# Attention with scores made twice: GpSimd sums all key chunks, a one-term score tile, moved rows of maxima, a front in three banks

## The chip, the cores and the metric

The kernel runs on 1 core of one Trainium2 chip. The metric is device time in microseconds (us) of one execution, shown as the median of several runs. The profile is one further execution with the hardware profiler on. Engines carry the profile's names: PE (TensorE), PEld (its weight loads), DVE (VectorE), ACT (ScalarE), POOL (GpSimd), SP (SyncE, which issues the transfers here).

## The reference

Attention with pooled queries, then a mixture of experts with Sinkhorn gating, then a soft mixture of experts. The change touches the attention alone:

```python
B, H, S, D = q.shape                       # 4, 8, 1152, 64
q_pool = q.reshape(B, H, S // 2, 2, D).mean(axis=3)
scores = (1.0 / np.sqrt(D)) * np.matmul(q_pool, k.transpose(0, 1, 3, 2))
scores = scores - np.max(scores, axis=-1, keepdims=True)
attn = np.exp(scores)
attn = attn / (np.sum(attn, axis=-1, keepdims=True) + 1e-09)
return np.matmul(attn, v)
```

## The kernel before, in words

There are 32 heads in 16 pairs. One head has 576 pooled queries and 1152 keys (9 chunks of 128). Scores are made twice. The first time (`emit_S`, queries on partitions, 384 keys a tile) serves only to find each query's maximum: a matmul, then a DVE maximum. A pair needs 9 query tiles: tile x = 0 holds the last 64 pooled queries of both heads, tiles 1 to 4 the others of one head, 5 to 8 those of the second; each takes three matmul groups. `emit_nm` negates and joins the three partial maxima; `emit_row` turns them by matmuls against the identity into a row that ACT copies into `q2`. The second time (`emit_E`, keys on partitions) scores of one chunk come out with the maximum already subtracted (two matmuls per half, one with `q1`, one with `q2`), and ACT takes the exponential into `e`. `emit_PV` multiplies by the values. The denominator is the sum of `e` over chunks (adds on POOL into `acc`, L223 and L225) and then over partitions (`emit_sum`: matmuls with ones).

Values are split into a rounded part and a remainder. `k_bank` transposes four chunks of keys, ACT copies the rounded part (L133), DVE subtracts for the remainder (L134); `q_bank` does so for queries (L104, L113, L115). `kq8` does the ninth chunk of keys and the last 64 queries, and fills `qd`, the weights of tile x = 0. `kd_dma` and `q2_dma` copy pieces to other partitions through SP's queue.

The order of work is written by hand (`manual_schedule`): a loop over slots, one chunk of one head each, 9 a head, 18 a pair (`u` is the slot within a pair, `nxt` and `nn` the pairs one and two ahead). Each slot makes exponentials for the present head and one score tile for a later one; even slots add the values' product of two chunks and a second score tile. Preparation of the coming pair, sums, rows and reciprocals hang at fixed `u`. All engines take their instructions in that order.

PSUM: two banks for the score tiles S, three for `se` (scores before the exponential), one bank `t` shared by all transposes, rows and sums (`bank()`), two for the product.

After slot 287 the experts' part begins, which this change does not touch.

Of the kernel before, what the change touches and what calls it, by code (L numbers as in the profile page):

```python
# [23 lines left out]
def attention(ctx, nc, tc, q, k, v, xa, ident, ones, hooks):  # L24
# [27 lines left out]

    qd = [kq_p.tile([128, 2, 128], F32R, name=f"qd{u}") for u in range(2)]

# [25 lines left out]
    def load_v(pi):  # L80
# [38 lines left out]
    def k_bank(pi, c0, n, ps):  # L119
        st = prep.setdefault(pi, {})  # L120
        if c0 == 0:
            st["kp"] = kq_p.tile([128, 2, 1152], F32R, tag="kp", name="kp")

            st["q1"] = kq_p.tile([128, 2, 2, 288], F32R, tag="q1", name="q1", bufs=2)
            st["q2"] = kq_p.tile([128, 2, 2, 288], F32R, tag="q2", name="q2", bufs=2)
        kr = raws["k"][pi]
        for c in range(n):
            nc.tensor.transpose(
                ps[:, c * 128:(c + 1) * 128], kr[:, c0 + c].rearrange("p h d -> p (h d)"), ident
            )  # L130
# [13 lines left out]
    def kq8(pi):  # L144
        ps = bank()
        k_bank(pi, 8, 1, ps)
        q_tr(pi, 8, 1, ps, 128)
        o, st = qd[pi % 2], prep[pi]
        xs = [(slice(64 * h, 64 * h + 64), slice(128 + 64 * h, 192 + 64 * h)) for h in range(2)]
        src = ps[:, 128:256].rearrange("p (h g x) -> p h g x", h=2, g=2)  # L150
        q1 = st["q1"][:, :, :, 256:]
        nc.scalar.copy(q1, src)
        for x, y in xs:
            nc.scalar.copy(o[x, 0, x], ps[x, y])
# [4 lines left out]
        for x, y in xs:  # L159
            nc.vector.tensor_tensor(out=o[x, 1, x], in0=ps[x, y], in1=o[x, 0, x].bitcast(F32), op=ALU.subtract)  # L160

# [8 lines left out]
    def q2_dma(pi):  # L170
        st = prep[pi]
        nc.sync.dma_start(out=st["q2"][0:64].bitcast(F32), in_=st["q1"][0:64].bitcast(F32))


    def emit_S(ph, x, n):
# [4 lines left out]
        if x == 0:  # L180
            mm = [(qd[pi % 2][:, z], st["kp"][:, 0]) for z in range(2)]
        else:
            g, u = divmod(x - 1, 2)
            mm = [(st["q1"][:, h, g, 128 * u:128 * u + 128], KD[ph % 3][:, 0])]
        ps = ps_s.tile([128, 512], F32, tag="S", name="S")[:, :384]
        for z, (w, r) in enumerate(mm):
            nc.tensor.matmul(ps, lhsT=w, rhs=r[:, 384 * n:384 * n + 384], start=z == 0, stop=z == len(mm) - 1)  # L187
        nc.vector.tensor_reduce(out=M_[ph][:, x, n:n + 1], in_=ps, axis=AX.X, op=ALU.max)  # L188
# [20 lines left out]
    def emit_E(ph, c):  # L209
# [11 lines left out]
        if c == 1:  # L221
            acc_[ph] = sm_p.tile([128, 2, 288], F32, tag="acc", name="acc")
            nc.gpsimd.tensor_tensor(out=acc_[ph], in0=E_[ph, 0], in1=e, op=ALU.add)  # L223
        elif 1 < c < 8:
            nc.gpsimd.tensor_tensor(out=acc_[ph], in0=acc_[ph], in1=e, op=ALU.add)  # L225

    def emit_PV(ph, c):
# [3 lines left out]
        for g in range(2):  # L231
# [3 lines left out]
            )  # L235
        if c < 8:
            E_.pop((ph, c))

    def emit_sum(ph):
        ps = bank()  # L240
        for z, t in enumerate((acc_.pop(ph), E_.pop((ph, 8)))):
            for g in range(2):
                nc.tensor.matmul(
                    ps[64 * g:64 * g + 64, :288], lhsT=ones[:, :64], rhs=t[:, g], start=z == 0, stop=z == 1
                )
        R_[ph] = sm_p.tile([128, 288], F32, tag="rs", name="rs")
# [18 lines left out]
    load_k(0)  # L265
    load_q(0)
    k0(0)
    k4(0)
    pool_q(0, 0)
    pool_q(0, 1)  # L270
    kq8(0)
    with tc.issue_after(kd_dma(0, 0)):
        load_k(1)
        kd_dma(0, 1)
        load_v(0)
# [8 lines left out]

    first(3)
    q_bank(0, 0)
    q_bank(0, 1)
    q2_dma(0)
    emit_nm(0, 0, 1)
    emit_row(0, 0, 1)  # L290
    first(12)
    pool_q(1, 0)
    pool_q(1, 1)
    emit_nm(0, 1, 4)
    k0(1)
    first()
    emit_row(0, 1, 4)

    for s in range(SLOTS * NPH + 9):
# [37 lines left out]
        if ph and c in (5, 6):  # L339
            emit_recip(ph - 1, c - 5)  # L340
        if ph + 1 < NPH:
            if u == 8 and ph + 2 < NPH:
                emit_nm(ph + 2, 0, 1)
            if u == 10:
                emit_row(ph + 1, 0, 1)
            if u in (6, 16):
                emit_nm(ph + 1, 1, 4)
            if u in (8, 17):
                emit_row(ph + 1, 1, 4)
        if ph and c == 7:  # L350
# [769 lines left out]
```

## Time and profile before

| | us |
|---|---|
| median of 3 runs | 2327.2 (2326.01 to 2327.26) |
| the profiled execution's own time | 2326.89 |
| span of its trace | 2324.9 |
| first exponential's scores begin (PE) | 33.31 |
| last sum of the attention begins (PE) | 607.88 |

The attention fills the first quarter of the span, the experts the rest. The page gives busy time for each engine over the whole span, so an average over unlike stages; the timeline gives, for each instruction, its start, its length and the engine's idle time before it with what ended it. Matmuls overlap, so on PE the distance from start to start says what an instruction costs.

### The profile page before, as it was taken

To read this page: it belongs to the slowest core of one execution; us is meant where nothing else is said; L and a number is where in the kernel's file an instruction comes from. 1 tells how busy PE (TensorE), PEld (TensorE's weight loads), DVE (VectorE), ACT (ScalarE), POOL (GpSimd) and SP (SyncE) were. 2 spreads that over 40 slices of the span, in tenths; PEclk is the share of its full clock that TensorE was granted. 3 is DMA by queue.
4 is the path that set the end of the run, shared out by engine and by line. 5 is a ranking of instruction groups with operands and counts; after the bars stand their busy time and mean duration, and the time that the engine had idled before them with its cause. 6 is when DMAs were issued, how large, how long until landed. Compare 5 with 4: busy or idle time off the path is not lost.

```text
span 2324.9 us, 41275 instructions
## 1 busy us (share of the span) xinstructions
PE 2218.8 (95%) x16965; PEld 1986.0 (85%) x16965; DVE 1446.5 (62%) x2692; ACT 843.0 (36%) x1779; POOL 538.8 (23%) x336
## 2 busy tenths in 40 slices
PE   6999999989999999999999999999999999999996
PEld 4666666666699999999999999999999999988863
DVE  5666666766667686686568558657755865622321
ACT  3454545544443442233334224223323423312212
POOL 4666666665500030030012003002100300100000
PEclk9999999999999999999999999999999999999998
DMA  7444354444121221121121212212211211221169
GB/s 169 104 101 118 92 122 109 92 109 136 32 74 46 91 91 56 55 100 56 64 82 65 73 55 83 82 40 88 82 46 64 92 64 56 103 98 55 55 221 313
DMA packets 121195, 211.40 MB, mean 91 GB/s; under 512 B 43696, under 2 KB 95408, under 8 KB 109744
## 3 DMA queue, kind: packets, MB, share of 16 engines
q1 hardware_dynamic: 121008, 208.77, 29.6%
q8 instruction: 134, 2.20, 0.4%
q14 instruction: 53, 0.43, 0.1%
HBM read 161.56 MB, written 14.16 MB: 76 GB/s over the span
## 4 chain that ended last, share of the span: by engine, by line
PE 59%; issue 8%; DVE 7%; ACT 1%; DMA 0%; POOL 0%; SPq 0%; DVEq 0%; ACTq 0%; POOLq 0%
PE g L550 9%; PE g L551 9%; PE g L552 9%; PE y L579 7%; PE y L577 7%; PE y L578 7%; DVE ho L539 2%; DVE ht L532 2%; PE y L649 1%; DVE v L470 1%; PE y L651 1%; PE y L650 1%; DVE acc L587 1%; PE se L216 1%; PE o L232 1%
## 5 line engine op out<-in xcount | busy, mean ns | idle before, releaser
L550 PE MATMUL g<-xs,w 128*128 128x256 f32 x2304 | 659.6, 286 | 0.0
L552 PE MATMUL g<-xs,w 128*128 128x256 f32 x2304 | 653.7, 284 | 1.0 <-DVE w L445 1.0
L551 PE MATMUL g<-xs,w 128*128 128x256 f32 x2304 | 654.0, 284 | 0.0
L577 PE MATMUL y<-v,ho 128*128 128x256 f32 x1764 | 503.3, 285 | 9.1 <-ACT ho L538 9.1
L579 PE MATMUL y<-v,ho 128*128 128x256 f32 x1764 | 503.2, 285 | 7.1 <-DVE ho L539 7.1
L578 PE MATMUL y<-v,ho 128*128 128x256 f32 x1764 | 502.1, 285 | 0.0
L550 PEld LDWEIGHTS g<-xs,w 128*128 128x128 f32 x2304 | 444.6, 193 | 7.7 <-issue 7.0
L552 PEld LDWEIGHTS g<-xs,w 128*128 128x128 f32 x2304 | 444.2, 193 | 1.2 <-DVE w L445 1.2
L551 PEld LDWEIGHTS g<-xs,w 128*128 128x128 f32 x2304 | 444.5, 193 | 0.3
L566 ACT ACTIVATE hr<-g 128x512 f32<-128x512 f32 x252 | 150.5, 597 | 772.6 <-PE g L552 753.5
L532 DVE TENSOR_TENSOR ht<-hr 128x512 f32<-128x512 f32 x315 | 230.1, 764 | 223.5 <-ACT hr L566 221.1
L577 PEld LDWEIGHTS y<-v,ho 128*128 128x128 f32 x1764 | 341.2, 193 | 10.4 <-ACT ho L538 10.4
L579 PEld LDWEIGHTS y<-v,ho 128*128 128x128 f32 x1764 | 341.8, 194 | 8.5 <-DVE ho L539 8.5
L445 POOL TENSOR_TENSOR w<-stg,w 128x1024 fp32r<-128x1024 f32 x28 | 68.1, 2433 | 1193.1 <-ACT w L444 1193.1
L578 PEld LDWEIGHTS y<-v,ho 128*128 128x128 f32 x1764 | 341.5, 194 | 0.0
L188 DVE TENSOR_REDUCE m<-S 128x1 f32<-128x384 f32 x432 | 235.2, 551 | 144.4 <-PE S L187 132.7
L587 DVE SCALAR_TENSOR_TENSOR acc<-y,P,acc 128x256 f32<-128x256 f32 x540 | 244.4, 477 | 117.4 <-PE y L579 117.4
L225 POOL TENSOR_TENSOR acc<-acc,e 128x576 f32<-128x576 f32 x192 | 273.7, 1425 | 98.7 <-ACT e L219 91.7
L539 DVE TENSOR_TENSOR ho<-ht,ho 128x512 fp32r<-128x512 f32 x315 | 258.5, 821 | 7.0 <-ACT ho L538 6.9
L219 ACT ACTIVATE e<-se 128x288 f32<-128x288 f32 x576 | 206.7, 410 | 144.3 <-PE se L216 141.3
L216 PE MATMUL se<-q,kd 128*128 128x288 f32 x1152 | 223.5, 311 | 15.7 <-ACT q L206 15.2
L538 ACT CAST ho<-ht 128x512 fp32r<-128x512 f32 x315 | 188.8, 618 | 81.3 <-DVE ht L532 78.6
(180 smaller groups left out, 2421.4 us busy)
## 6 DMA issues: line engine op xcount, KB each, us to landing
xs<-xd SPq DMA_DIRECT2D x63, 1024.0 KB, 4.8
stg<-in_moe_w_dram SPq DMA_DIRECT2D x60, 512.0 KB, 5.9
kd<-kp SPq DMA_DIRECT2D x32, 576.0 KB, 5.7
m2w<-in_moe_w_dram SPq DMA_DIRECT2D x13, 1024.0 KB, 10.4
m2w<-in_moe_w_dram SPq DMA_DIRECT2D x22, 512.0 KB, 8.7
kr<-in_k_dram SPq DMA_DIRECT2D x32, 288.0 KB, 6.4
qr<-in_q_dram SPq DMA_DIRECT2D x16, 576.0 KB, 3.8
kd<-kp SPq DMA_DIRECT2D x32, 288.0 KB, 3.2
```

What stands on the lines that cost most here:

```text
L188: nc.vector.tensor_reduce(out=M_[ph][:, x, n:n + 1], in_=ps, axis=AX.X, op=ALU.max)
L216: nc.tensor.matmul(ps, lhsT=kd[:, z, 128 * c:128 * c + 128], rhs=y[:, h, g], start=z == 0, stop=z == 1)
L225: nc.gpsimd.tensor_tensor(out=acc_[ph], in0=acc_[ph], in1=e, op=ALU.add)
L532: nc.vector.tensor_tensor(out=src, in0=q[0], in1=q[1], op=op)
L539: nc.vector.tensor_tensor(out=o[:, 1], in0=src, in1=o[:, 0].bitcast(F32), op=ALU.subtract)
L550: nc.tensor.matmul(o, lhsT=w[:, 0, kk, c], rhs=x[:, 0, kk], start=kk == 0, stop=False)
L551: nc.tensor.matmul(o, lhsT=w[:, 0, kk, c], rhs=x[:, 1, kk], start=False, stop=False)
L552: nc.tensor.matmul(o, lhsT=w[:, 1, kk, c], rhs=x[:, 0, kk], start=False, stop=kk == 3)
L577: nc.tensor.matmul(ps, lhsT=o[:, 0, c], rhs=v[:, 0, c], start=c == 0, stop=False)
L578: nc.tensor.matmul(ps, lhsT=o[:, 0, c], rhs=v[:, 1, c], start=False, stop=False)
L579: nc.tensor.matmul(ps, lhsT=o[:, 1, c], rhs=v[:, 0, c], start=False, stop=c == 3)
L587: nc.vector.scalar_tensor_tensor(out=y, in0=ps, scalar=p, in1=y, op0=ALU.mult, op1=ALU.add)
```

## The change

- `qd` keeps only the rounded part: tile x = 0 is one matmul instead of two, and two DVE subtractions a pair go.
- In `kq8` the query transpose comes before the copies of the key part of the bank instead of after them.
- The ninth chunk's `e` is added into `acc` by POOL too; `emit_sum` is two matmuls instead of four.
- `emit_row` stands right behind the slot's exponentials and first score tile, instead of at the slot's end.
- `k0`, `k4` move from u = 14, 16 to 13, 15, `q_bank(nxt, 0)` from 5 to 6 (first pair: `kq8` to 3, `k0(1)`, `k4(1)` into slots 1 and 2).
- In the front the first pair's banks come from the three `se` banks; queries are pooled first, both `q_bank`s come before the score tiles, all 15 tiles of head 0 come before its rows, and `q2_dma` and both `kd_dma` are issued before the next pair's loads.

The order in which the engines get their work, by program text. PE, slots 7 to 9 of a pair (`se` scores of a chunk, `S` score tiles, `o` values' product, `t<-identr,nm` the row of maxima). Before:

```order
L187 MATMUL S<-kp,qd_123 128x384 x2
L216 MATMUL se<-q_2218,kd_126 128x288
...
L187 MATMUL S<-kp,qd_123 128x384 x2
L232 MATMUL o<-e,vr 64x288 x4
L187 MATMUL S<-kp,qd_123 128x384 x2
L200 MATMUL t<-identr,nm_125 128x128 x4
L216 MATMUL se<-q_2218,kd_127 128x288
L216 MATMUL se<-q_2219,kd_127 128x288
```

With the change:

```order
L189 MATMUL S<-kp,qd_123 128x384
L218 MATMUL se<-q_2166,kd_126 128x288
...
L189 MATMUL S<-kp,qd_123 128x384
L202 MATMUL t<-identr,nm_125 128x128 x4
L234 MATMUL o<-e,vr 64x288 x4
L189 MATMUL S<-kp,qd_123 128x384
L218 MATMUL se<-q_2166,kd_127 128x288
L218 MATMUL se<-q_2167,kd_127 128x288
```

The row moved ahead of the values' product and of one score tile, and each tile of x = 0 is one matmul.

DVE, slots 5 to 8 of a pair (`q<-t,q` the remainder of a bank of queries, `m` maxima of a score tile, `nm` their join, `rs` reciprocals). Before:

```order
L115 TENSOR_TENSOR q_2218<-t,q_2218 64x256 x2
L251 RECIPROCAL rs<-rs 128x144
L188 TENSOR_REDUCE m_2289<-S 128x1 x2
L251 RECIPROCAL rs<-rs 128x144
L191 TENSOR_REDUCE nm_125<-m_2289 128x4
L188 TENSOR_REDUCE m_2469<-S 128x1
```

With the change:

```order
L250 RECIPROCAL rs<-rs 128x144
L190 TENSOR_REDUCE m_2251<-S 128x1
L120 TENSOR_TENSOR q_2166<-t,q_2166 64x256 x2
L190 TENSOR_REDUCE m_2251<-S 128x1
L250 RECIPROCAL rs<-rs 128x144
L193 TENSOR_REDUCE nm_125<-m_2251 128x4
L190 TENSOR_REDUCE m_2427<-S 128x1
```

The queries' remainder moved behind the first reciprocal and one maximum; the join `nm` stands where it stood.

POOL, one pair (`acc` sums of `e`, `qp` the pooled queries of the pair after next). Before:

```order
L100 TENSOR_TENSOR qp<-qr 128x9x64 x2
L223 TENSOR_TENSOR acc<-e 128x576
L225 TENSOR_TENSOR acc<-acc,e 128x576 x6
L223 TENSOR_TENSOR acc<-e 128x576
L225 TENSOR_TENSOR acc<-acc,e 128x576 x6
```

With the change:

```order
L105 TENSOR_TENSOR qp<-qr 128x9x64 x2
L225 TENSOR_TENSOR acc<-e 128x576
L227 TENSOR_TENSOR acc<-acc,e 128x576 x7
L225 TENSOR_TENSOR acc<-e 128x576
L227 TENSOR_TENSOR acc<-acc,e 128x576 x7
```

The ninth chunk's add now stands ahead of the pooling of queries.

The diff, cut to its core:

```diff
-    qd = [kq_p.tile([128, 2, 128], F32R, name=f"qd{u}") for u in range(2)]
+    qd = [kq_p.tile([128, 128], F32R, name=f"qd{u}") for u in range(2)]
...
+    front = [True]
     def bank():
+        if front[0]:
+            return ps_e.tile([128, 512], F32, tag="se", name="t")
         return ps_t.tile([128, 512], F32, tag="t", name="t")
...
+        if n == 1:
+            q_tr(pi, 8, 1, ps, 128)
         o = st["kp"][:, 0, c0 * 128:(c0 + n) * 128]
...
         k_bank(pi, 8, 1, ps)
-        q_tr(pi, 8, 1, ps, 128)
...
-        for x, y in xs:
-            nc.vector.tensor_tensor(out=o[x, 1, x], in0=ps[x, y], in1=o[x, 0, x].bitcast(F32), op=ALU.subtract)
...
-        for z, (w, r) in enumerate(mm):
-            nc.tensor.matmul(ps, lhsT=w, rhs=r[:, 384 * n:384 * n + 384], start=z == 0, stop=z == len(mm) - 1)
+        nc.tensor.matmul(ps, lhsT=w, rhs=r[:, 384 * n:384 * n + 384], start=True, stop=True)
...
-        elif 1 < c < 8:
+        elif c > 1:
             nc.gpsimd.tensor_tensor(out=acc_[ph], in0=acc_[ph], in1=e, op=ALU.add)
...
-        for z, t in enumerate((acc_.pop(ph), E_.pop((ph, 8)))):
-            for g in range(2):
-                nc.tensor.matmul(
-                    ps[64 * g:64 * g + 64, :288], lhsT=ones[:, :64], rhs=t[:, g], start=z == 0, stop=z == 1
-                )
+        t = acc_.pop(ph)
+        for g in range(2):
+            nc.tensor.matmul(ps[64 * g:64 * g + 64, :288], lhsT=ones[:, :64], rhs=t[:, g], start=True, stop=True)
...
     load_q(0)
+    pool_q(0, 0)
+    pool_q(0, 1)
     k0(0)
     k4(0)
-    pool_q(0, 0)
-    pool_q(0, 1)
     kq8(0)
-    with tc.issue_after(kd_dma(0, 0)):
+    kd_dma(0, 0)
+    q_bank(0, 0)
+    q_bank(0, 1)
+    with tc.issue_after(q2_dma(0)):
+        kd_dma(0, 1)
         load_k(1)
-        kd_dma(0, 1)
...
-    first(3)
-    q_bank(0, 0)
-    q_bank(0, 1)
-    q2_dma(0)
+    first(15)
     emit_nm(0, 0, 1)
+    emit_nm(0, 1, 4)
     emit_row(0, 0, 1)
-    first(12)
+    emit_row(0, 1, 4)
+    front[0] = False
+    first()
...
         first()
+        if ph + 1 < NPH:
+            if u in (8, 17):
+                emit_row(ph + 1, 1, 4)
+            if u == 10:
+                emit_row(ph + 1, 0, 1)
         if on and nxt < NPAIR:
-            if s == 0:
-                k4(1)
-            if u == (2 if s < 9 else 1):
+            if s in (1, 2):
+                (k0, k4)[s - 1](1)
+            if u == (3 if s < 9 else 1):
...
-            elif u == 5:
+            elif u == 6:
                 q_bank(nxt, 0)
...
-            if u == 14:
+            if u == 13:
                 k0(nn)
-            elif u == 16:
+            elif u == 15:
                 k4(nn)
```

## Rows read from the trace of the kernel before

**Rows 1.** The page, part 1: busy us, share of the span, instructions of each engine.
```profile
PE 2218.8 (95%) x16965; PEld 1986.0 (85%) x16965; DVE 1446.5 (62%) x2692; ACT 843.0 (36%) x1779; POOL 538.8 (23%) x336
```

**Rows 2.** Stretches: start:end, length, busy us (count) by engine, PEclk, DMA share, GB/s.
```profile
33.31:609.00 575.69, 530.36 (x3428) 369.39 (x3428) 379.77 (x814) 289.04 (x775) 358.45 (x253) 1.00 0.44 106
540.00:545.00 5.00, 4.46 (x18) 2.63 (x19) 1.97 (x6) 1.40 (x3) 1.37 (x2) 0.66 0.00 0
```

**Rows 3.** Timeline of one pair, PE: start us, length, line, count [idle before, releaser].
```profile
285.47 0.34 PE L216 MATMUL se<-q,kd 128*128 128x288 f32 x1
...
300.07 0.70 PE L216 MATMUL se<-q,kd 128*128 128x288 f32 x4
301.17 0.62 PE L187 MATMUL S<-kp,qd 128*128 128x384 f32 x2 [0.40 <-DVE m L188]
302.15 0.51 PE L187 MATMUL S<-kp,qd 128*128 128x384 f32 x2
...
304.56 0.34 PE L216 MATMUL se<-q,kd 128*128 128x288 f32 x1
305.40 0.67 PE L216 MATMUL se<-q,kd 128*128 128x288 f32 x3 [0.49 <-ACT q L206]
...
311.42 0.66 PE L243 MATMUL t<-acc,ones 128*64 128x288 f32 x4
311.90 0.66 PE L243 MATMUL t<-e,ones 128*64 128x288 f32 x4
...
321.12 0.63 PE L200 MATMUL t<-identr,nm 128*128 128x128 f32 x4 [0.56 <-DVE nm L191]
321.59 0.34 PE L216 MATMUL se<-q,kd 128*128 128x288 f32 x1
...
325.29 0.27 PE L128 MATMUL t<-ident,kr 128*128 128x128 f32 x1
326.52 0.30 PE L104 MATMUL t<-ident,qp 128*128 128x128 f32 x1 [0.95 <-DVE kp L134]
```

**Rows 4.** Timeline of the same pair, DVE, POOL and ACT.
```profile
298.69 0.77 DVE L115 TENSOR_TENSOR q<-t,q 64x256 fp32r<-64x256 f32 x2 [0.50 <-ACT q L113]
...
301.50 1.04 DVE L251 RECIPROCAL rs<-rs 128x144 f32<-128x144 f32 x1
...
302.46 0.11 DVE L191 TENSOR_REDUCE nm<-m 128x4 fp32r<-128x12 f32 x1
...
317.60 2.90 POOL L225 TENSOR_TENSOR acc<-acc,e 128x576 f32<-128x576 f32 x2 [0.55 <-ACT e L219]
...
320.16 0.71 ACT L219 ACTIVATE e<-se 128x288 f32<-128x288 f32 x2 [1.17 <-PE se L216]
...
320.47 2.78 POOL L100 TENSOR_TENSOR qp<-qr 128x576 f32<-128x576 f32 x2
```

**Rows 5.** Timeline of the front, SP and PE.
```profile
12.40 0.50 SPq L166 DMA_DIRECT2D kd<-kp  x1
...
22.31 0.95 PE L187 MATMUL S<-kd,q 128*128 128x384 f32 x2
...
32.40 1.11 PE L200 MATMUL t<-identr,nm 128*128 128x128 f32 x4 [1.12 <-DVE kp L134]
```

**Rows 6.** The page, part 6: transfers, KB each, median us from issue to landing.
```profile
kd<-kp SPq DMA_DIRECT2D x32, 576.0 KB, 5.7
```

**Rows 7.** Timeline of the attention's end, POOL and PE.
```profile
601.78 5.88 POOL L225 TENSOR_TENSOR acc<-acc,e 128x576 f32<-128x576 f32 x4 [0.75 <-ACT e L219]
...
607.88 0.66 PE L243 MATMUL t<-acc,ones 128*64 128x288 f32 x4
```

**Rows 8.** Groups by line and shape, 0 to 640 us: busy us, mean ns | idle before.
```profile
L461 POOL TENSOR_TENSOR vs<-vb 128x1024 f32<-128x1024 f32 x1 | 3.3, 3345 | 0.0
L461 POOL TENSOR_TENSOR va<-vb,va 128x1024 f32<-128x1024 f32 x1 | 2.4, 2403 | 0.1
L100 DVE TENSOR_TENSOR qp<-qr 128x576 f32<-128x576 f32 x2 | 1.4, 750 | 0.0
```

More of the change, by code (lines that the diff above doesn't have):

```diff
@@ L146, in kq8 @@
         k_bank(pi, 8, 1, ps)
-        q_tr(pi, 8, 1, ps, 128)
         o, st = qd[pi % 2], prep[pi]
-        xs = [(slice(64 * h, 64 * h + 64), slice(128 + 64 * h, 192 + 64 * h)) for h in range(2)]
         src = ps[:, 128:256].rearrange("p (h g x) -> p h g x", h=2, g=2)
         q1 = st["q1"][:, :, :, 256:]
+        for h in range(2):
+            nc.scalar.copy(o[64 * h:64 * h + 64, 64 * h:64 * h + 64], ps[64 * h:64 * h + 64, 128 + 64 * h:192 + 64 * h])
         nc.scalar.copy(q1, src)
-        for x, y in xs:
-            nc.scalar.copy(o[x, 0, x], ps[x, y])
         for h in range(2):
@@ L158, in kq8 @@
             )
-        for x, y in xs:
-            nc.vector.tensor_tensor(out=o[x, 1, x], in0=ps[x, y], in1=o[x, 0, x].bitcast(F32), op=ALU.subtract)
     def kd_dma(pi, h):
@@ L171, in q2_dma @@
         st = prep[pi]
-        nc.sync.dma_start(out=st["q2"][0:64].bitcast(F32), in_=st["q1"][0:64].bitcast(F32))
+        return nc.sync.dma_start(out=st["q2"][0:64].bitcast(F32), in_=st["q1"][0:64].bitcast(F32)).ins
     def emit_S(ph, x, n):
@@ L180, in emit_S @@
         if x == 0:
-            mm = [(qd[pi % 2][:, z], st["kp"][:, 0]) for z in range(2)]
+            w, r = qd[pi % 2], st["kp"][:, 0]
         else:
             g, u = divmod(x - 1, 2)
-            mm = [(st["q1"][:, h, g, 128 * u:128 * u + 128], KD[ph % 3][:, 0])]
+            w, r = st["q1"][:, h, g, 128 * u:128 * u + 128], KD[ph % 3][:, 0]
         ps = ps_s.tile([128, 512], F32, tag="S", name="S")[:, :384]
-        for z, (w, r) in enumerate(mm):
-            nc.tensor.matmul(ps, lhsT=w, rhs=r[:, 384 * n:384 * n + 384], start=z == 0, stop=z == len(mm) - 1)
+        nc.tensor.matmul(ps, lhsT=w, rhs=r[:, 384 * n:384 * n + 384], start=True, stop=True)
         nc.vector.tensor_reduce(out=M_[ph][:, x, n:n + 1], in_=ps, axis=AX.X, op=ALU.max)
@@ L235, in emit_PV @@
             )
-        if c < 8:
-            E_.pop((ph, c))
+        E_.pop((ph, c))
     def emit_sum(ph):
         ps = bank()
-        for z, t in enumerate((acc_.pop(ph), E_.pop((ph, 8)))):
-            for g in range(2):
-                nc.tensor.matmul(
-                    ps[64 * g:64 * g + 64, :288], lhsT=ones[:, :64], rhs=t[:, g], start=z == 0, stop=z == 1
-                )
+        t = acc_.pop(ph)
+        for g in range(2):
+            nc.tensor.matmul(ps[64 * g:64 * g + 64, :288], lhsT=ones[:, :64], rhs=t[:, g], start=True, stop=True)
         R_[ph] = sm_p.tile([128, 288], F32, tag="rs", name="rs")
@@ L283, in first @@
                 emit_S(*firsts.pop(0))
-    first(3)
-    q_bank(0, 0)
-    q_bank(0, 1)
-    q2_dma(0)
+    first(15)
     emit_nm(0, 0, 1)
+    emit_nm(0, 1, 4)
     emit_row(0, 0, 1)
-    first(12)
+    emit_row(0, 1, 4)
+    front[0] = False
+    first()
     pool_q(1, 0)
     pool_q(1, 1)
[L294 to L297, printed above, removed]
     for s in range(SLOTS * NPH + 9):
@@ L340, in attention @@
             emit_recip(ph - 1, c - 5)
[L341 to L349, printed above, removed]
+        if u == 8 and ph + 2 < NPH:
+            emit_nm(ph + 2, 0, 1)
+        if u in (6, 16) and ph + 1 < NPH:
+            emit_nm(ph + 1, 1, 4)
         if ph and c == 7:
```

## The prediction

> **What bounds the kernel now.** The page comes first: PE is busy for 95% of the span [rows 1], but that mixes the experts, which are not touched, with the attention. So I cut out the attention: in 575.69 us PE is busy 530.36, DVE 379.77, POOL 358.45, ACT 289.04 [rows 2]. PE leads there and yet is not full, and no other engine is near its limit. A stage like this is read from one pair in the timeline. A pair takes 321.59 - 285.47 = 36.12 us [rows 3]. On PE the instructions stand head to tail except at five places, and these are what the reader should look for: a score tile that waits for DVE's maxima (301.17), two waits for ACT's copy of the row (305.40, and the same again behind 321.59), a row that waits for the joined maxima (321.12) and the ninth query transpose, which waits until DVE has read another part of the same bank (326.52) [rows 3]. So the attention's time is PE's work plus these waits, and each edit is worth what it takes from one or the other. I count from start to start, since the ends of matmuls are modelled; four `se` matmuls stand (0.70 - 0.34) / 3 = 0.12 us apart [rows 3].
>
> **The sum, term by term.** It is made against the profiled execution, 2326.9 us, which lies 0.3 below the median.
>
> 1. *Sums of two matmul groups instead of four.* The first half starts at 311.42, the second at 311.90 [rows 3]: 0.48 us of PE for each head goes, 32 x 0.48 = **-15.4**. The price is one more add on POOL (term 4).
> 2. *Tile x = 0 with one matmul.* Two take 0.51 us, and a single one's length in that pair is 0.34 by the same model (two start 0.17 apart) [rows 3]. Three a pair; the first pair's lie in the front, where other things decide. 45 x 0.17 = **-7.7**. The two DVE subtractions that go with it lie in idle time of DVE: nothing.
> 3. *Ninth query transpose ahead of the copies.* From the key transpose to the query transpose 326.52 - 325.29 = 1.23 us pass; back to back I take 0.12, as for `se`. 15 x 1.11 = **-16.7**.
> 4. *The add ahead of the pooling.* That transpose reads the pooled queries, so term 3 holds only if POOL is there in time. Now the last add of the odd head ends at 317.60 + 2.90 = 320.50 and the pooling runs to 323.25. With the change the ninth add can start when ACT has the last exponential, 320.16 + 0.71 = 320.87; 1.45 for the add (2.90 for two) and 2.78 for the pooling end it at 325.10 [rows 4]. The query transpose could start at 325.29 + 0.12 = 325.41 [rows 3]. A cover of 0.3 us: I take **0**. Bounds: 0, and the whole of term 3 (+16.7) where POOL is 1.4 us late. This also says what a shorter wait at 321.12 would bring: PE would reach the transpose early and wait for POOL there.
> 5. *Row at u = 8 ahead of the values' product.* From 304.56 to 305.40 are 0.84 us instead of 0.12: with the product of two chunks between row and use, ACT's copy is hidden. 16 x 0.72 = **-11.5**. The row at u = 17 stays right before its use, and that wait stays.
> 6. *Queries' bank at u = 6 instead of 5.* The tile at 301.17 waits because DVE sat 0.50 us for ACT's copy (298.69) and then did subtraction and reciprocal before the maxima [rows 4]. With the reciprocal first, that idle time goes. From the four matmuls at 300.07 the next would start after about 0.53; it started after 1.10: 15 x 0.57 = **-8.6**. Bounds: 0 and this.
> 7. *A new wait, in the row at u = 8.* Its old place was behind the product; its new one is just behind the slot's score tile: 302.15 less 0.57 (term 6) less one 0.17 (term 2), plus the tile's own 0.17, about 301.6. The joined maxima are ready at 302.46 + 0.11 = 302.57 [rows 4], less the 0.50 of idle time that goes, 302.07. So PE waits about 0.5, and the product and the next tile queue behind the row: 15 x 0.5 = **+7.5**. Bounds: 0, and 1.04 more (one reciprocal, the instruction ahead of the join [rows 4]).
> 8. *`k0` and `k4` a slot earlier.* I looked whether the wait at 321.12 goes. DVE has the same two subtractions, two reciprocals and maxima between the tile of slot 14 and the join, only in another order, and runs through them without a pause; the row's place on PE doesn't move either. **0**. Bounds: -0.56 x 15 = -8.4, most of which POOL would take back (term 4), and +3.
> 9. *The front.* Tiles from x = 1 on need the second copy of keys to other partitions, issued 12.40 to 12.90 [rows 5]; with 5.7 us to landing [rows 6] it is there at about 18.1. Before, these tiles began at 22.31 because both banks of queries stood between. With the change the banks come first and the tiles begin as soon as the copy lands: 4.2 earlier. The head's rows no longer wait 1.12 us for the next pair's keys (32.40) [rows 5]; in return those keys' transposes, about as long as the row's 1.11, are paid inside slot 1. Together **-4**. Bounds: 0 (the queue lands the copy later, since the order of loads changed) and -6.
> 10. *The end.* POOL's adds for the last head run without pause to 607.66, and the last sum starts at 607.88 [rows 7]. Now the sum needs one more add, 1.45 us, while PE is there earlier by what terms 1 and 5 save in the last two heads: **+0.9**. Bounds 0 and 2.
>
> Sum: -15.4 - 7.7 - 16.7 + 0 - 11.5 - 8.6 + 7.5 + 0 - 4 + 0.9 = **-55.5**, so 2326.9 - 55.5 = 2271.4, rounded to **2271 us**.
>
> A rule that speaks against the change: the Trainium skill, GPSIMD Engine Reference, section Performance versus the Vector engine, says that GpSimd needs about twice as long as VectorE for plain elementwise work and that such work belongs on VectorE. The trace agrees about the lengths: pooling 128x576 takes 750 ns on DVE [rows 8] and 2.78 / 2 = 1.39 us on POOL [rows 4]. By the rule the ninth add would sit on DVE, 32 x 0.75 = 24 us more there, and where DVE is late (terms 6 and 7) it would be paid, so up to 24 us less gain; by the rows POOL has room and DVE doesn't, and I leave the sum as it is.
>
> **The rivals.**
>
> *A. POOL is late at the pair's border.* The cover in term 4 is 0.3 us out of a chain of 4.2. For it: spans on POOL are rough, and a shorter pair pushes the adds together. Against it: POOL shows idle time before the adds (0.55 us at 317.60 [rows 4]). If it is 0.5 us too late, 15 x 0.5 = 7.5 us go, 2279; at the bound 2288.
>
> *B. DVE is late.* PE shortens its pair by 3 us, DVE's work shrinks little, so waits for maxima come back. If term 7 is as large as a whole reciprocal more (15 x 0.54 = 8) or term 6 gives nothing (8.6), the time is 2279 to 2280; with both, 2288. For it: the waits at 301.17 and 321.12 are already DVE's.
>
> *C. Slower than before: adds and DVE disturb each other.* POOL's work a pair becomes 16 x 1.45 + 2.78 = 26.0 us, of a new pair of 36.12 - 3.4 = 32.7. Rows show one kind of POOL add at 2403 ns and at 3345 ns, a factor of 1.39 [rows 8]. By that factor POOL would need 36.1 us a pair, as long as the pair is now; above it POOL is the bound and the kernel slower. At 1.45 a pair takes 37.7: 16 x 1.6 - 4 = +21, 2348. Against it: the adds beside a reciprocal (317.60 and 301.50) show 1.45 us and nothing near 2 [rows 4]. The Trainium skill, GPSIMD Engine Reference, section Specifications, states such a contention, for VectorE instructions with two SBUF inputs or in a two-port mode.
>
> *D. PE's granted clock.* One stretch of the attention shows 0.66 (540 to 545 [rows 2]), about 5 x 0.34 = 1.7 us lost. A denser PE may do without it or a stretch may be added: 2269 or 2273. That is within the forecast's own width.
>
> *E. The saved work comes back as waits in the same place and nothing changes.* Terms 1 and 2 are work that is not issued any more, by the order shown; for no change every wait would have to grow by its whole saving.
>
> **How the numbers follow.** A measurement of this kernel can tell about 0.2% (4.7 us) from no change. Forecast with D: 0.57 (2262 to 2279). A: 0.19. B: 0.16. C: 0.04. E: 0.02. Below 2260: 0.02. For the range I go to terms 7 and 9 at their good ends (-7.5 and -2, and the clock's -1.7: 2260) and to A or B at their bounds (2288), a little wider on both sides: 2258 to 2290. Faster by over 0.2% are the forecast, A, B and the lower tail, 0.94; same 0.02; slower 0.04.
>
> **What would show it.** In the profile after: a pair of about 32.7 us; 128 rows of `t<-acc,ones` as before and none from `e`; 48 matmuls with `qd` instead of 96; no wait of the query transpose for L134's line, and if one appears, it names POOL or the pooling (A); the row at u = 8 with a wait of about 0.5 us for `nm`, and no wait of 0.49 at the `se` behind it; the row at u = 17 as before; the first exponential's scores at about 28 us; the last sum waiting for POOL by about 1 us. I am wrong if the pair takes 34 us or more, if POOL's adds lengthen beyond 1.5 us, or if a wait of `S` for `m` of more than 0.3 us a pair remains.

## The result, and the profile after

| | before | after |
|---|---|---|
| median (4 runs each) | 2326.78 us (2326.01 to 2327.26) | 2275.39 us (2274.2 to 2276.38) |
| profiled execution, its own time | 2326.89 | 2275.54 |
| span of its trace | 2324.9 | 2273.7 |
| first exponential's scores begin | 33.31 | 27.23 |
| first matmul of the experts begins | 608.95 | 555.66 |

The ratio is 0.9779 with a 95% interval of 0.9762 to 0.9796: 51 us faster. 2271 was forecast, with a range of 2258 to 2290, so the time lies 4.4 us above the forecast. The rest of this text asks whether it came out of the steps named, and where the 4.4 us are.

The page of the changed kernel, part 1 (busy us, share of the span, instructions), answers to [rows 1]:

```profile
PE 2191.6 (96%) x16789; PEld 1970.6 (87%) x16789; DVE 1436.3 (63%) x2660; ACT 841.7 (37%) x1779; POOL 583.8 (26%) x368
```

176 matmuls less, 128 of the sums and 48 of tile x = 0, and 32 more adds on POOL: the change does what it says. The stretches (start:end, length, busy us and count by engine, PEclk, DMA share, GB/s) answer to [rows 2]: the attention, and two short stretches within it.

```profile
27.23:555.66 528.43, 504.90 (x3258) 354.82 (x3257) 372.91 (x786) 288.55 (x776) 405.76 (x287) 0.99 0.50 118
95.00:100.00 5.00, 5.00 (x29) 3.03 (x29) 1.93 (x5) 1.64 (x8) 2.63 (x3) 0.76 0.43 123
325.00:330.00 5.00, 4.96 (x23) 3.45 (x24) 1.58 (x4) 1.65 (x5) 2.84 (x3) 0.66 0.22 55
```

The attention takes 528.43 us instead of 575.69, and PE is busy for 504.90 / 528.43 = 96% of it instead of 92%. Two stretches have a low granted clock where before there was one; they come back below.

One pair on PE (start us, length, engine, line, operation, count [idle before, what ended it]) answers to [rows 3]:

```profile
256.57 0.69 PE L218 MATMUL se<-q,kd 128*128 128x288 f32 x4
257.37 0.44 PE L189 MATMUL S<-kd,q 128*128 128x384 f32 x1
258.12 0.63 PE L202 MATMUL t<-identr,nm 128*128 128x128 f32 x4 [0.31 <-DVE nm L193]
258.59 0.34 PE L218 MATMUL se<-q,kd 128*128 128x288 f32 x1
259.42 0.66 PE L218 MATMUL se<-q,kd 128*128 128x288 f32 x3 [0.49 <-ACT q L208]
...
262.29 0.27 PE L133 MATMUL t<-ident,kr 128*128 128x128 f32 x1
262.40 0.27 PE L109 MATMUL t<-ident,qp 128*128 128x128 f32 x1
...
267.35 0.66 PE L244 MATMUL t<-acc,ones 128*64 128x288 f32 x4
267.94 0.44 PE L189 MATMUL S<-kd,q 128*128 128x384 f32 x1
...
271.69 0.70 PE L218 MATMUL se<-q,kd 128*128 128x288 f32 x4
272.23 0.34 PE L189 MATMUL S<-kp,qd 128*128 128x384 f32 x1
...
273.05 0.34 PE L189 MATMUL S<-kp,qd 128*128 128x384 f32 x1
273.82 0.63 PE L202 MATMUL t<-identr,nm 128*128 128x128 f32 x4 [0.44 <-DVE nm L193]
...
275.51 0.45 PE L189 MATMUL S<-kp,qd 128*128 128x384 f32 x1
275.79 0.69 PE L218 MATMUL se<-q,kd 128*128 128x288 f32 x4
...
291.40 0.35 PE L218 MATMUL se<-q,kd 128*128 128x288 f32 x1
```

A pair takes 291.40 - 258.59 = 32.81 us instead of 36.12. Of the five waits to look for before, three are gone: the score tile in u = 7 follows the scores at 271.69 after 0.54 us (272.23) instead of 1.10, the query transpose comes 0.11 us behind the key transpose instead of 1.23, and at u = 8 nothing waits for the copy of the row any more, as behind the tile at 275.51 the scores follow after 0.28 us. In its place the row at 273.82 waits for the join, 0.77 us from start to start where 0.17 would do. At the pair's border the row still waits for the join (258.12) and the scores still for the copy (259.42, 0.83 us).

The same pair's border on POOL, and the slots 6 to 8 on DVE, answer to [rows 4]:

```profile
259.31 2.79 POOL L105 TENSOR_TENSOR qp<-qr 128x576 f32<-128x576 f32 x2
...
271.21 0.77 DVE L120 TENSOR_TENSOR q<-t,q 64x256 fp32r<-64x256 f32 x2
...
272.60 1.05 DVE L250 RECIPROCAL rs<-rs 128x144 f32<-128x144 f32 x1
273.57 0.11 DVE L193 TENSOR_REDUCE nm<-m 128x4 fp32r<-128x12 f32 x1
```

The queries' remainder has lost its idle time of 0.50 us [rows 4], as forecast. The second reciprocal, begun at 272.60, holds the join back to 273.57, and PE is there first. POOL ends the pooling at 259.31 + 2.79 = 262.10, and the transpose that reads it starts at 262.40: the cover of term 4 is 0.30 us, exactly as worked out.

The front and the end, on PE, answer to [rows 5] and [rows 7]:

```profile
16.90 0.98 PE L189 MATMUL S<-kd,q 128*128 128x384 f32 x2 [1.72 <-DMA kd<-kp]
...
27.23 1.55 PE L218 MATMUL se<-q,kd 128*128 128x288 f32 x4
...
555.03 0.71 PE L244 MATMUL t<-acc,ones 128*64 128x288 f32 x4 [1.14 <-POOL acc L227]
```

The tiles from x = 1 on begin at 16.90 (18.1 forecast), as the copy lands, and the last sum waits 1.14 us for POOL's ninth add (about 1 forecast).

### The profile page after: what moved, and what is told of

The parts are those of the page before. It is cut to its first block, busy times and chain, and to the rows that moved or that the text cites. A ratio compares the mean times of both kernels' runs of the same rounds, so it can differ in the third digit from the quotient of the medians.

```text
span 2273.7 us, 40984 instructions
## 1 busy us (share of the span) xinstructions
PE 2191.6 (96%) x16789; PEld 1970.6 (87%) x16789; DVE 1436.3 (63%) x2660; ACT 841.7 (37%) x1779; POOL 583.8 (26%) x368
## 4 chain that ended last, share of the span: by engine, by line
PE 74%; DVE 13%; issue 9%; ACT 1%; DMA 1%; POOL 1%; SPq 0%; ACTq 0%; DVEq 0%; POOLq 0%
PE g L548 10%; PE g L549 10%; PE g L550 10%; PE y L577 7%; PE y L576 7%; PE y L575 7%; PE o L234 6%; PE se L218 5%; PE S L189 4%; DVE rs L250 3%; DVE m L190 2%; DVE ho L537 2%; DVE ht L530 2%; PE y L647 2%; PE y L649 1%
## 5 line engine op out<-in xcount | busy, mean ns | idle before, releaser
L227 POOL TENSOR_TENSOR acc<-acc,e 128x576 f32<-128x576 f32 x224 | 318.7, 1423 | 73.8 <-ACT e L221 64.5
```

## The experiments

Each run is timed beside the kernel before. The edits are against the changed kernel. First the changed kernel itself, as a base.

> The changed kernel once more, nothing edited: 2275 us, within 2 us. What it is for: in its first trace the granted clock was below 1.00 near 95, 327, 577, 600 and 795 us, in that of the kernel before near 542, 630 and 850. Theory: these stretches belong to the single execution, so they fall elsewhere here and the pairs of the attention that held them (34.4 us) take 32.8. Rival: they belong to the new order of work, then they fall at the same places again.

2274.58 us (2273.25 to 2276.96); ratio 0.9778, 0.9765 to 0.9791. Differences below are against this median, and a pair of 32.80 us in its trace. In the attention the granted clock is low in two stretches again: one has moved (290 to 295 us instead of 95 to 100), the other lies once more at 320 to 330. So neither the theory nor its rival is borne out whole. The halves of a pair that hold them take 17.24 and 17.27 us, 1.54 and 1.57 longer than their like.

### The terms that were to pay: sums, transpose, one-term tile, front

**Four matmul groups in the sums again**, the ninth add off POOL:

```diff
-        elif c > 1:
+        elif 1 < c < 8:
...
-        t = acc_.pop(ph)
-        for g in range(2):
-            nc.tensor.matmul(ps[...], lhsT=ones[:, :64], rhs=t[:, g], start=True, stop=True)
+        for z, t in enumerate((acc_.pop(ph), E_.pop((ph, 8)))):
+            for g in range(2):
+                nc.tensor.matmul(ps[...], lhsT=ones[:, :64], rhs=t[:, g], start=z == 0, stop=z == 1)
```

> The changed kernel with the ninth chunk's add taken off GpSimd again and the sum over partitions made of four matmul groups, as before. Theory: PE is head to tail there, so the 0.48 us per head come back and the last sum no longer waits about 1.1 us for GpSimd: +15.4 - 1 = +14, 2290 us, a pair of 33.8 us. Rival 1: the added adds had cost something elsewhere (GpSimd late), then less than +10 comes back. Rival 2: the matmuls had lain beside other waits, then the time stays at 2275 to 2278.

2285.86 us, +11.3, and a pair of 33.73, +0.93: the two groups cost their 0.47 us a head in each pair, as term 1 has it. That the total moves by less than 15 pairs' worth (14.0) is in keeping with the last sum, which no longer waits for POOL, and with the granted clock: summed over windows of 5 us, 5 x (1 - granted clock) is 1.7 us in the attention and 13.5 in the experts (counted up to 2100 us) of this trace, and 3.4 and 15.3 in the base's. (This sum is called the clock's loss below. It is an estimate from above, since it counts a stretch whole, also where PE would have waited.)

**The query transpose behind the copies again:**

```diff
-        if n == 1:
-            q_tr(pi, 8, 1, ps, 128)
...
         k_bank(pi, 8, 1, ps)
+        q_tr(pi, 8, 1, ps, 128)
```

> The changed kernel with the ninth query transpose behind the copies of the key part again. Theory: the wait of 1.1 us comes back in each pair, 15 x 1.1 = +16.7, 2292 us, a pair of 33.9 us with one start-to-start gap of 1.22 on PE. Rival: the transpose now waits for GpSimd's pooling in part, so that undoing the move gives back less than 10 us.

2290.46 us, +15.9; ratio 0.9846, 0.9832 to 0.9859; a pair of 33.96, +1.16. The wait is back in its old size, 1.22 us from start to start, in PE's timeline of this kernel:

```profile
269.28 0.27 PE L133 MATMUL t<-ident,kr 128*128 128x128 f32 x1
270.50 0.30 PE L109 MATMUL t<-ident,qp 128*128 128x128 f32 x1 [0.96 <-DVE kp L139]
```

**Two matmuls and two subtractions for tile x = 0 again** (the rounded and the remaining part in `qd`):

```diff
-            w, r = qd[pi % 2], st["kp"][:, 0]
+            mm = [(qd[pi % 2][:, z], st["kp"][:, 0]) for z in range(2)]
...
+            nc.vector.tensor_tensor(out=o[x, 1, x], in0=ps[x, y], in1=o[x, 0, x].bitcast(F32), op=ALU.subtract)
```

> The changed kernel with tile x = 0 made of two matmuls again, and its two subtractions on VectorE. Theory: of the three extra matmuls of 0.17 us a pair, two stand ahead of the row at u = 8, which waits 0.60 us for the join there, and lie within that wait; only the third is paid: 15 x 0.17 = +2.6, 2278 us, and the row's wait falls to about 0.26. Rival, as the sum before the result had it: all three are paid, +7.7, 2283.

2282.05 us, +7.5, and a pair of 33.36, +0.56: the whole of term 2 (7.7) is paid. I had expected less, as the row at u = 8 waits anyway and two of the three matmuls stand ahead of it. That wait did shrink, but the subtractions made a new one for the first score tile at u = 3, where there was none (PE's timeline of this kernel):

```profile
271.41 0.44 PE L193 MATMUL S<-kd,q 128*128 128x384 f32 x1 [0.23 <-DVE m L194]
```

So in this denser pair the subtractions do not lie in idle time, as they did in the kernel before: DVE's queue is late there.

**The front of before** (banks from the one shared bank, `q_bank`s behind the first tiles, pooling behind `k4`):

```diff
-    front = [True]
+    front = [False]
...
-    kd_dma(0, 0)
-    q_bank(0, 0)
-    q_bank(0, 1)
-    with tc.issue_after(q2_dma(0)):
+    with tc.issue_after(kd_dma(0, 0)):
         load_k(1)
+        kd_dma(0, 1)
...
-    first(15)
+    first(3)
+    q_bank(0, 0)
+    q_bank(0, 1)
+    q2_dma(0)
...
-            if s in (1, 2):
-                (k0, k4)[s - 1](1)
+            if s == 0:
+                k4(1)
```

> The changed kernel with the front of before (one bank, keys first, three tiles, then queries, rows in two parts, the next pair's keys partly ahead of the loop). Theory: the first exponential's scores start at about 33 us instead of 27, and the first pair has 0.7 us less to do: +5.4, 2280 us. Rival, the front is hidden behind the transfers that both need: +2 or less.

2278.83 us, +4.3, with a pair of 32.80 as in the base. The first exponential's scores begin 6.2 us later than in the base's trace, where they begin at 26.61 (PE's timeline of this kernel). Term 9 said 4. Behind the first pair the two traces are 5.7 us apart; that the median shows less may be the clock's loss, 17.1 us here (attention and experts) and 18.7 in the base's.

```profile
32.78 0.55 PE L218 MATMUL se<-q,kd 128*128 128x288 f32 x1
```

### How thin is POOL's cover, and would VectorE do the add better?

**One spare add of 1.41 us on POOL ahead of the pooling:**

```diff
             if u == 17:
+                qr = raws["q"][nn]
+                nc.gpsimd.tensor_tensor(out=spare[:, :, 0, :], in0=qr[:, :, 0, :], in1=qr[:, :, 1, :], op=ALU.add)
                 pool_q(nn, 0)
```

> The changed kernel with one spare add of 128x576 (1.41 us, its result unused) on GpSimd ahead of each pooling. Theory: GpSimd's cover at the ninth query transpose is 0.30 us, so 1.1 us a pair become a wait of TensorE there: 14 x 1.1 = +15.5, 2291 us. Rival, the cover is larger or the wait is taken back by the waits that follow in the pair: 2275 to 2282.

2290.19 us, +15.6. PE's timeline of this kernel:

```profile
268.40 0.27 PE L134 MATMUL t<-ident,kr 128*128 128x128 f32 x1
269.63 0.33 PE L110 MATMUL t<-ident,qp 128*128 128x128 f32 x1 [0.96 <-POOL qp L106]
```

The transpose comes 1.23 us behind the key transpose instead of 0.11, so of the 1.41 us added 1.12 show and 0.29 were covered. Fifteen times 1.12 is 16.8. So rival A's mechanism is real, POOL becomes late where term 4 put it, and the change stops 0.3 us short of that.

**The ninth add on VectorE instead, one slot later:**

```diff
+    def emit_ninth(ph):
+        nc.vector.tensor_tensor(out=acc_[ph], in0=acc_[ph], in1=E_[ph, 8], op=ALU.add)
...
+        if ph and c == 1:
+            emit_ninth(ph - 1)
```

> The changed kernel with the ninth chunk's add on VectorE instead of GpSimd, one slot after that chunk's exponential. Theory: an add takes about 0.75 us there instead of 1.42 and stands where VectorE has room, so little changes: 2274 to 2277; the last sum waits less (-0.5 to -1). Rival 1: VectorE's queue is the tight one, and the add pushes its maxima back by 0.75 us twice a pair: up to +24, 2290 and more. Rival 2: GpSimd's relief gives something: below 2272.

2301.07 us, +26.5, with a pair of 34.46: far worse than expected, on the rival's side. The timeline of this kernel, three of DVE's 32 adds and what POOL does around them:

```profile
273.20 1.40 POOL L225 TENSOR_TENSOR acc<-e 128x576 f32<-128x576 f32 x1 [4.06 <-ACT e L221]
273.58 1.65 DVE L241 TENSOR_TENSOR acc<-acc,e 128x576 f32<-128x576 f32 x1
...
558.64 4.43 POOL L227 TENSOR_TENSOR acc<-acc,e 128x576 f32<-128x576 f32 x3 [0.59 <-ACT e L221]
563.15 0.76 DVE L241 TENSOR_TENSOR acc<-acc,e 128x576 f32<-128x576 f32 x1
566.00 1.41 POOL L225 TENSOR_TENSOR acc<-e 128x576 f32<-128x576 f32 x1 [2.94 <-ACT e L221]
...
577.00 2.34 POOL L464 TENSOR_TENSOR vs<-va,vb 128x1024 f32<-128x1024 f32 x1
577.08 2.88 DVE L241 TENSOR_TENSOR acc<-acc,e 128x576 f32<-128x576 f32 x1 [3.61 <-POOL acc L227]
```

The add at 563.15 has POOL idle beside it (558.64 + 4.43 = 563.07, next 566.00) and takes 0.76 us. The one at 273.58 starts while POOL adds, and ends at 275.23, which is 0.63 after POOL's end at 274.60. The one at 577.08 starts beside a longer POOL instruction and takes 2.88: it ends at 579.96, 0.62 after POOL's end at 579.34. Of the 32 adds, the 31 that start inside a POOL instruction all end 0.60 to 0.63 us after that instruction's end, whenever they started. So VectorE does not run slower beside GpSimd, it stands still until the GpSimd add is over, and the GpSimd add under way keeps its 1.40 to 1.42 us. The Trainium skill, SBUF — State Buffer, section SBUF: two separate sides, says that a VectorE instruction with two SBUF inputs and a GpSimd instruction that reads SBUF take their common ports as an exclusive lock, and that the one that comes second is fully blocked: these 31 rows agree, for the case in which GpSimd came first. Rows for the other case stand below, with rival C.

How the longer add reaches PE is in the rows behind it. ACT's copies into `qd` wait for DVE's subtraction of the keys, which stands behind the add, and the exponentials queue behind the copies (timeline of the same kernel, ACT and PE):

```profile
275.46 0.42 ACT L158 CAST qd<-t 64x64 fp32r<-64x64 f32 x2 [1.98 <-DVE kp L141]
...
276.53 0.53 PE L218 MATMUL se<-q,kd 128*128 128x288 f32 x2 [0.89 <-ACT e L221]
```

The place matters, then: by the row at 563.15 an add on VectorE where GpSimd is idle would take 0.76 us. Such a place was not tried, so the run does not show what the ninth add would cost there.

### The row at u = 8: a wait gone, a wait made

**The row at u = 8 back at its slot's end:**

```diff
-            if u in (8, 17):
+            if u in (17,):
                 emit_row(ph + 1, 1, 4)
...
+        if u == 8 and ph + 1 < NPH:
+            emit_row(ph + 1, 1, 4)
```

> The changed kernel with the row at u = 8 at the end of its slot again, behind the product and the second score tile. Theory: the move exchanged one wait for another. The 0.71 us wait for ACT's copy comes back (16 x 0.71 = 11.4) and the 0.60 us wait for the join goes (15 x 0.60 = 9.0): +2.4, 2278 us. Rival 1, the move paid in full and the join's wait has another cause (it stays): +11, 2287. Rival 2, the move cost as much as it gave: 2275 or less.

2275.68 us, +1.1; ratio 0.9782, 0.9769 to 0.9796, not told apart from the base's 0.9778. The pair is 32.93, +0.13. Terms 5 and 7 both exist: the wait for ACT's copy is back in full, 0.83 us, and the row itself no longer waits (PE's timeline of this kernel).

```profile
276.37 0.56 PE L202 MATMUL t<-identr,nm 128*128 128x128 f32 x4
276.76 0.35 PE L218 MATMUL se<-q,kd 128*128 128x288 f32 x1
277.59 0.66 PE L218 MATMUL se<-q,kd 128*128 128x288 f32 x3 [0.49 <-ACT q L208]
```

Moving the row, alone, exchanges 0.72 us for 0.60: 2 us over 15 pairs. That the median shows 1.1 and not more may be the clock's loss, which is 1.7 and 13.6 in this trace and so 3.4 less than in the base's.

**The second reciprocal one slot later, behind the join:**

```diff
-        if ph and c in (5, 6):
-            emit_recip(ph - 1, c - 5)
...
+        if ph and c in (5, 7):
+            emit_recip(ph - 1, (c - 5) // 2)
```

> The changed kernel with the second of the two reciprocals (1.04 us of VectorE) moved one slot later, behind the join of the maxima that the rows wait for. Theory: both row waits are VectorE's queue, so the 0.60 us at u = 8 and the 0.86 us at u = 17 (0.58 in the row, 0.28 in the tile ahead of it) go; but TensorE then reaches the ninth query transpose 0.86 earlier, GpSimd's cover there is 0.30, and 0.56 comes back as a wait for the pooling: 15 x (0.60 + 0.30) = -13.5, 2262 us, a pair of 31.9. Rival 1, GpSimd is not close: -22, 2253. Rival 2, the waits have another cause (TensorE's own queue, the copy): 2273 to 2276.

2262.78 us, -11.8; ratio 0.9727, 0.9714 to 0.974, and a pair of 32.23, -0.57. The row at u = 8 no longer waits, so the wait of term 7 was made by the reciprocal ahead of the join, and not by the maxima. The pairs explain 15 x 0.57 = 8.6 of the 11.8; the clock's loss is 0 in the attention and 13.5 in the experts of this trace, 5.2 less than in the base's, which is more than the 3.2 left. So the time came out as expected (2262) in part by luck: the pair was to fall to 31.9.

**In addition the pooling at u = 13 and 15**, since in the run before POOL's pooling had come 0.2 us late for the shorter pair:

```diff
-            if u == 17:
-                pool_q(nn, 0)
-                pool_q(nn, 1)
+            if u in (13, 15):
+                pool_q(nn, (u - 13) // 2)
```

> As the run before, and the pooling of the pair after next goes to u = 13 and 15 instead of both parts at u = 17, so that it is done before the ninth add. Theory: the wait of 0.56 us for the pooling goes too: 15 x (0.60 + 0.86) = -22, 2253 us, a pair of 31.3; the sum over partitions comes four slots after its last add and is not held up. Rival: GpSimd's adds fall behind in the odd head (14.2 us of work in some 15 us), the sum or the values' product waits, and the gain stays at that of the run before or is smaller.

2257.34 us (2256.12 to 2258.89); ratio 0.9703, 0.969 to 0.9717. It beats both kernels, by 17.2 us the changed one. A pair takes 31.97, and not the 31.3 expected. What is left of waits in it, PE's timeline of this kernel:

```profile
250.25 0.63 PE L202 MATMUL t<-identr,nm 128*128 128x128 f32 x4 [0.24 <-DVE nm L193]
...
251.56 0.66 PE L218 MATMUL se<-q,kd 128*128 128x288 f32 x3 [0.49 <-ACT q L208]
...
265.19 0.33 PE L189 MATMUL S<-kp,qd 128*128 128x384 f32 x1
265.36 0.56 PE L202 MATMUL t<-identr,nm 128*128 128x128 f32 x4
```

At u = 8 the row follows the tile at once; at the border the row's wait for the join and the scores' wait for the copy remain.

**Two attempts at the border's waits.** First score tiles two further ahead, so that the row can go to u = 16 (not shown: the second bank of keys goes from u = 15 to 17):

```diff
-    first()
+    first(3)
...
-            if u in (8, 17):
+            if u in (8, 16):
...
-        if u in (6, 16) and ph + 1 < NPH:
+        if u in (5, 15) and ph + 1 < NPH:
```

> As the run with the join first and the pooling early, and the score tiles run two further ahead (three instead of one behind the first rows), so that both joins come one slot earlier, the row at u = 17 goes to u = 16 ahead of the values' product, and the second bank of keys to u = 17. Theory: the wait for the copy at the pair's start (0.70 us) is hidden as at u = 8, the row's wait for the join (0.40) goes, and two tiles in the front cost 1.3: 15 x -1.1 + 1.3 = -15, 2242 us, a pair of 30.9. Rival: the one bank that rows, keys and queries share or VectorE's queue makes new waits, the gain is under 5 us.

2287.6 us, 30 above the run before, with a pair of 33.60: a miss by 45 us, and of the wrong sign. PE's timeline of this kernel:

```profile
253.08 0.44 PE L189 MATMUL S<-kd,q 128*128 128x384 f32 x1 [0.61 <-DVE q L120]
...
261.15 0.63 PE L202 MATMUL t<-identr,nm 128*128 128x128 f32 x4 [0.78 <-DVE nm L193]
```

The row at u = 16 waits longer than the one at 17 did (0.78 us instead of 0.24), and tiles of S wait for DVE's queue. The pairs explain 15 x (33.60 - 31.97) = 24.5 of the 30 us; the granted clock was also low from 15 to 35 and from 495 to 505 us, where that of the run before was not. Running ahead on PE did not help while DVE was late. Which of the four moves in this edit made DVE late was not separated.

Then, at u = 0, the scores of chunk 0 behind the product and the second score tile, so that these cover the copy:

```diff
-        if on:
+        late = on and s and u == 0
+        if on and not late:
             emit_E(ph, c)
...
+        if late:
+            emit_E(ph, c)
```

> Kernel: the second reciprocal behind the join, the pooling at u=13 and 15 (as in the run before that took 2257.3 us), and in addition the scores of chunk 0, at the first slot of a pair, go behind the values' product and the second score tile of that slot. Theory (at u=0 TensorE stands still until the copies of the queries are made, 0.83 us start to start for a group of 0.13, and other work put there covers it): of the 0.70 us some 0.4 is won, the rest comes back as the chunk's exponential starts later; 15 pairs x 0.4 = 6, so 2251 us and a pair of 31.6 us. Rival (the exponentials of chunk 0 and 1 now follow each other closely, and the next sum or values' product waits for ScalarE instead): nothing is won or it is slower, 2257 us or more.

2261.94 us, +4.6 on the run without it, and a pair of 287.39 - 255.24 = 32.15 instead of 31.97. The copy is hidden, the scores run without a break from 255.52, but a tile now waits for DVE (timeline of this kernel, DVE and PE):

```profile
254.62 1.65 DVE L190 TENSOR_REDUCE m<-S 128x1 f32<-128x384 f32 x3
255.24 0.44 PE L189 MATMUL S<-kd,q 128*128 128x384 f32 x1 [0.56 <-DVE m L190]
255.52 1.52 PE L218 MATMUL se<-q,kd 128*128 128x288 f32 x8
...
287.39 0.44 PE L189 MATMUL S<-kd,q 128*128 128x384 f32 x1 [0.57 <-DVE m L190]
```

Three maxima follow head to tail at 254.62, behind a reciprocal (from 252.46) and four products with the reciprocals: the score tiles had come together, and DVE was late with them. Neither theory named this: the exponentials, on which the rival was laid, were not the wait.

## Why the prediction was right, and by how much its terms were off

| term | forecast, us | measured, us | from |
|---|---|---|---|
| 1 sums | -15.4 | -15.4 | 267.35 to 267.94: 0.59 a sum, the 0.48 of the second half [rows 3] gone |
| 2 tile x = 0 | -7.7 | -7.5 | the run with two terms (its pair: 15 x 0.56 = 8.4) |
| 3 query transpose | -16.7 | -16.8 | 15 x (1.23 - 0.11) |
| 4 add ahead of pooling | 0 | 0 | cover 0.30; 0.29 by the spare add |
| 5 copy at u = 8 | -11.5 | -11.5 | comes back as 0.83 in the run with the row at the end |
| 6 queries' bank | -8.6 | -8.4 | 15 x (1.10 - 0.54), the tile at the head of u = 7 |
| 7 new wait of the row | +7.5 | +9.0 | 15 x (0.77 - 0.17) |
| 8 `k0`, `k4` earlier | 0 | +1.8 | 15 x 0.12, the waits alone, below |
| 9 front | -4 | -5.4 | first scores 6.1 earlier, the first pair gains 0.7 less than the others; -4.3 by the run |
| 10 end | +0.9 | +1.1 | last sum's idle time |
| sum | -55.5 | -53.1 | |

The first matmul of the experts comes 608.95 - 555.66 = 53.3 us earlier, and the last instruction 51.2 us earlier.

**The steps that held.** Terms 1, 3, 4, 5, 6 and 10 came out within 0.3 us each, those of which a run undid one (1, 3, and 4's cover) with the size forecast in the pair. Rivals A and B did not decide: POOL was in time by 0.3 us, no tile lost what term 6 gave, and the new wait of term 7 was 0.1 us larger a pair, not a whole reciprocal. E fell at once, with the pair 3.3 us shorter. (What hides term 4 was tested by the spare add alone; terms 6, 8 and 10 are read from the trace, and no run undid them.)

**Right in size, by another split when undone: term 2.** In the kernel before, the two subtractions cost PE nothing, as the prediction had it: the tile at 293.26 follows the scores at 292.74 by 0.52 us. In the denser pair they would cost, by the run with two terms as a wait at u = 3, while the matmuls at u = 7 and 8 are partly covered by the row's wait. The two happen to cancel, so that run's 7.5 us do not show the three matmuls by themselves.

**Off in size: terms 7, 8 and 9.** The new wait of term 7 is 0.60 us a pair where 0.5 was forecast, and the front gave 1.4 us more than term 9 had. In term 8 the prediction said that the wait at the border stays, because the same work stands ahead of the join on DVE. The wait did split: the row now waits 0.75 - 0.17 = 0.58 us, but the tile ahead of it, which follows the scores at 256.57 by 0.80 us instead of 0.54, waits 0.26 where it did not wait before. Together 0.84 instead of the 0.89 - 0.17 = 0.72 of before, so 0.12 a pair, within its bound of +3. (The tile's 0.26 is also the wait of `S` for `m` that the prediction named as a sign of being wrong above 0.3.) The term looked at waits alone and left out what it does on PE. Slots 13 to 16, which hold the key transposes, take 289.38 - 282.69 = 6.69 us from start to start where they took 319.69 - 312.77 = 6.92: the transposes now stand ahead of scores and not ahead of the values' product. Term 6 has the reverse of this: slots 5 and 6, with the queries' transposes, take 271.69 - 268.22 = 3.47 instead of 300.07 - 296.73 = 3.34. Together that gives 0.10 a pair, 1.5 us that no term had.

**What the sum left out.** The experts were taken as untouched in time as well. 53.3 - 51.2 = 2.1 us are given back there. The clock's loss allows for up to 1.7 of it, 15.3 us in the experts after and 13.6 before; the rest was not traced. In the attention it is 3.4 instead of 1.7, the two stretches of the profile against the one [rows 2]. The prediction had 1.7 as rival D, within the forecast's own width; what it left out is that the experts have such stretches too.

**The account.** Up to the experts the terms give 53.1 us and the transposes' places 1.5, and the second clock stretch takes back 1.6 (a pair that holds one takes 34.37 us instead of 32.80): 53.0 of the 53.3 measured. With the 2.1 given back in the experts this leaves 51.2, and 2326.89 - 2275.54 = 51.4 by the times of the profiled executions. So the 4.1 us missing of the 55.5 forecast are terms 7 and 8, a clock stretch and the experts, less what the transposes and the front gave beyond the sum.

**The rival on the other side, C.** Its mechanism is there, but as a wait of the one that comes second, and it hardly occurs in the pairs. GpSimd's adds were to lengthen; in the mean they stayed at 1.42 us, as the group of the adds into `acc` shows (page of the changed kernel, part 5: busy us, mean ns | idle before):

```profile
L227 POOL TENSOR_TENSOR acc<-acc,e 128x576 f32<-128x576 f32 x224 | 318.7, 1423 | 73.8 <-ACT e L221 64.5
```

The subtractions and products of the pairs on DVE have one operand in PSUM, and the products of 64x256 took 419 ns in the means of both kernels. Two instructions with both inputs in SBUF do fall into the attention, work for the experts in one of its last pairs, and each lengthens a GpSimd add that begins while it runs. One of the two, in the timeline of the changed kernel:

```profile
485.38 1.23 DVE L483 TENSOR_TENSOR xs<-x,xs 128x1024 fp32r<-128x1024 f32 x1 [0.26 <-ACT xs L482]
486.11 1.77 POOL L227 TENSOR_TENSOR acc<-acc,e 128x576 f32<-128x576 f32 x1 [0.82 <-ACT e L221]
```

The add ends 1.27 us after VectorE's end at 486.61, and takes 1.77 us instead of 1.42; the other (at 469.55) takes 2.23 and ends 1.27 us after VectorE's end as well. So when VectorE comes first it is GpSimd that stands still. C's factor of 1.39 [rows 8] is such a wait and not a stretch, in the timeline of the kernel before:

```profile
619.53 3.42 DVE L470 TENSOR_TENSOR v<-va,v 128x1024 fp32r<-128x1024 f32 x1
621.83 3.35 POOL L461 TENSOR_TENSOR vs<-vb 128x1024 f32<-128x1024 f32 x1
```

VectorE ends at 622.95 and GpSimd 2.23 us later, where the other one of its kind took 2.40 us in all [rows 8]. By these rows C could not come about by denser work alone: it needs a VectorE instruction with both inputs in SBUF in each pair, which the change does not add. For the same reason the rule that was weighed, from the Trainium skill, GPSIMD Engine Reference, section Performance versus the Vector engine, does not carry here: by the lengths of [rows 8] the ninth add on VectorE costs 0.75 us. The bound of 24 us worked out from that came near the 26.5 measured, but what made the add 1.85 us was the wait for GpSimd and not VectorE's own work.

## What to carry to other kernels

Cost an edit by the wait that ends last behind it, and then look at what runs ahead of the waiter: of the 17 us that were still to be had here, 9 by the pairs (12 by the median) lay in one reciprocal in front of a join. Moving a matmul earlier bought little here, as its operand was made by an in-order queue that was late: moving the row alone brought 1 to 2 us, moving the reciprocal out of its operand's way the 9. Before moving an elementwise add from GpSimd to VectorE, look whether GpSimd is idle where it will run: in this case, where it was not, VectorE waited out the GpSimd instruction whole, and everything queued behind it waited too. The other way round, the GpSimd adds that began during such a VectorE instruction waited for its end.

## What was not expected of the hardware

- **VectorE's add against GpSimd's.** An add of 128x576 with both inputs in SBUF takes 0.76 us beside an idle GpSimd and ends 0.60 to 0.63 us after the GpSimd instruction in whose time it starts, in 31 of 31 cases; 2.88 us was the longest. A GpSimd add of that size that begins during a VectorE instruction with two SBUF inputs ends 1.27 us after it (1.77 and 2.23 us instead of 1.42, both cases in the trace of the changed kernel).
- **TensorE's granted clock at the pair's border.** The attention is denser after the change (96% busy), and yet has two stretches below full clock instead of one: means of 0.76 and 0.66 over 5 us, so part of each at 1.2 GHz and the rest at 2.4. Both lie just behind a pair's border (rows of maxima at 92.40 and 323.73), where PE waits for the join and for the copy. The three runs with the join first and the score tiles where they were, in which PE waits less, have none in the attention; the run with the spare add, in which PE waits 1.1 us more a pair, has a clock's loss of 12.0 us there, of which the halves of pairs that hold such a stretch show some 0.4 us each. Which borders it falls on differs between executions: 95 to 100 and 325 to 330 us in one of the changed kernel, 290 to 295 and 320 to 330 in another. What decides that stays open.
